# A small spread read of w_mod issued behind c on ScalarE's queue, with DMA semaphores of its own

## The chip, the cores and the metric

One core of a Trainium2 chip runs the whole block. The metric is device time in microseconds (us) of one execution. Ratios are computed from the mean time of one kernel's fast runs over that of the other's fast runs of the same rounds on the same chip, so they are not quite the ratios of the medians quoted beside them. The granted TensorE clock does not count the slow start: in the kernel before it is 1.000 although the first matmuls run at half rate until 7.7 us.

## The reference

A transformer block of a diffusion model, bf16, with two images of 256 tokens, width 1152, two heads, MLP width 4608:

```
mod = (silu(c) @ w_mod).reshape(B, 6, 1, D)          # w_mod: 1152 x 6912
shift_a, scale_a, gate_a, shift_m, scale_m, gate_m = ...
h   = layernorm(x) * (1 + scale_a) + shift_a
qkv = h @ wqkv ;  a = softmax(q k^T / sqrt(Dh)) v @ wo ;  x = x + gate_a * a
h2  = layernorm(x) * (1 + scale_m) + shift_m
out = x + gate_m * (gelu(h2 @ w_fc1) @ w_fc2)
```

## The kernel before

A small scheduler writes each engine's instructions in a fixed order and sets the semaphore waits. The parts that the change and the argument touch are the loads at the start, the way in which DMAs get semaphores, and the tensor engine's (PE's) list at the start:

```
# emit: which semaphore counts a DMA (56 in all, the last 8 for ScalarE and GpSimd)
if e == "sp":
    k = di % n_sp ; di += 1
else:
    k = n_sp + dj % n_other ; dj += 1
...
# first loads: c on ScalarE's queue, all others on SyncE's (SP)
dma(CSB[0:18, :], c.rearrange("b (k p) -> (b k) p", p=P), 18 * 256, "ld_c", eng="act")
for b in range(2):
    dma(X[:, 2*b:2*b+2, :], xv[b], ..., "ld_x%d" % b)
for (ka, kb) in ((0, KC), (KC, KT)):                  # KC = 4, KT = 9
    for k0, k1 in ((0, 3), (3, 6), (6, 9)):           # columns of scale_a
        dma(WSC[:, k0:k1, ka*P:kb*P], wmod_v[:, k0:k1, D+ka*P:D+kb*P], ..., "ld_sc%d_%d" % (ka, k0))
    for kt in range(ka, kb):
        dma(WK[:, kt, :], wqkv_v[:, kt, D:2*D], ..., "ld_wk%d" % kt)    # key weights; the first waits for x1
...
# PE at the start: 5 dummies, transpose of c, then
warm(7, "b")                                          # dummies of 512 columns
for n, behind in ((1, "bn_ln1_1_1"), (1, "aggr_ln1_1"), (2, "veps_ln1_1"), (2, "rstd_ln1_1")):
    warm(n, behind, behind)                           # dummies that also wait for x's statistics
xn_T(1); sca(0, 3); warm(1, "d"); sca(3, 6); warm(1, "f", "aggr_ln1_2")
xn_T(0); sca(6, 9); xn_T(2, 0, 8)                     # transposes of x; scale_a from w_mod's three pieces
k_first(0); k_first(1); ...                           # the first key matmuls
```

The dummies keep PE busy so that its clock rises; they compute nothing.

## Time and profile before

| | before |
|---|---|
| time, median of the first 3 runs | 244.01 us (243.94 to 244.44) |
| span of the profiled run | 242.6 us |
| PE busy | 238.3 us (98%) |
| first key matmul | 11.55 us |
| first key weights issued, landed | 6.0, 11.4 us |

The views that carry the argument stand in the prediction. In a timeline row the first number is the start in us, the second the duration, and the bracket tells how long the engine was idle and what ended that. Matmuls are pipelined and their ends are modelled, so a wait of 0.1 us between matmuls shows only in the starts. Ends of transfers come from the view of one transfer at a time ("DMA to landing"), and counts of slow packets from the trace's packet records, which no view prints.

### The profile page before, as it was taken

The page shows a single profiled execution, that of the slowest core. Times are in us where ns is not written, and L with a number is a line of the kernel's source. Part 1 is how long each engine was busy: PE and PEld are TensorE (multiplying, and loading weights), DVE is VectorE, ACT ScalarE, POOL GpSimd, SP SyncE. Part 2 cuts the span into 40 slices and gives each one's busy share as a digit, 9 for nine tenths or more (in the row PEclk, how much of TensorE's full clock was granted, in tenths as well). Part 3 has the DMA queues.
Part 4 walks back from the last instruction along what each step waited for, and adds up shares of the span by engine and source line. Part 5 has one row for each costly group of instructions (what it writes and reads, how often), then busy time and mean ns, then how long its engine had stood idle before and what let it go on. Part 6 is the DMA issues. An engine that isn't in the chain of part 4 may idle for free.

```text
span 242.6 us, 3989 instructions
## 1 busy us (share of the span) xinstructions
PE 238.3 (98%) x1717; PEld 146.4 (60%) x1727; DVE 120.0 (49%) x216; ACT 66.9 (28%) x136; POOL 21.7 (9%) x39
## 2 busy tenths in 40 slices
PE   7999999999999999999999999999999999999996
PEld 2688854557667666898444444444565665665664
DVE  3824379596988799789999600000012222211112
ACT  4730350345424207983233332222000000000000
POOL 1500000000021186400000000020000000000000
PEclk9999999999999999999999999999999999999999
DMA  6999999999994999999943488002000000000001
GB/s 237 330 383 394 388 392 389 397 412 408 390 355 138 349 385 393 390 320 394 329 145 87 165 301 331 0 16 85 0 16 19 16 16 19 16 16 16 19 17 32
DMA packets 29995, 51.57 MB, mean 213 GB/s; under 512 B 1431, under 2 KB 15643, under 8 KB 29979
## 3 DMA queue, kind: packets, MB, share of 16 engines
q1 hardware_dynamic: 29536, 50.14, 57.8%
q0 software_dynamic: 416, 1.19, 1.6%
q8 instruction: 13, 0.21, 0.4%
q14 instruction: 3, 0.02, 0.0%
q10 hardware_dynamic: 27, 0.00, 0.0%
HBM read 50.14 MB, written 1.19 MB: 212 GB/s over the span
## 4 chain that ended last, share of the span: by engine, by line
PE 98%; issue 0%; POOL 0%; DVE 0%; POOLq 0%
PE psum L688 96%; PE psum L691 2%; POOL arena L713 0%; DVE arena L1289 0%; DVE arena L1290 0%; POOL arena L712 0%; POOL arena L719 0%; POOL arena L717 0%; POOLq L1351 0%
## 5 line engine op out<-in xcount | busy, mean ns | idle before, releaser
L688 PE MATMUL psum<-arena 128*128 128x384 bf16 (+9 forms) x1628 | 235.0, 310 | 2.0 <-POOL arena L713 1.5
L688 PEld LDWEIGHTS psum<-arena 128*128 128x128 bf16 (+1 forms) x1638 | 141.1, 97 | 91.8 <-issue 4.7
L1081 DVE SCALAR_TENSOR_TENSOR arena<-arena 128x1152 f32<-128x1152 bf16 x32 | 44.7, 1413 | 0.6
L1289 DVE TENSOR_TENSOR arena<-psum,arena 128x384 f32<-128x384 f32 (+2 forms) x13 | 6.9, 527 | 68.3 <-PE psum L688 68.3
L1197 ACT ACTIVATE arena<-psum 128x512 bf16<-128x512 f32 (+1 forms) x44 | 22.4, 519 | 42.7 <-PE psum L688 42.7
L683 ACT ACTIVATE arena<-psum 128x512 bf16<-128x512 f32 (+6 forms) x37 | 19.5, 549 | 39.8 <-PE psum L688 38.5
L685 DVE CAST arena<-psum 128x512 bf16<-128x512 f32 (+3 forms) x13 | 8.1, 639 | 11.5 <-PE psum L688 11.5
L669 POOL DMA_DIRECT2D dit_scratch<-arena x3 | 1.8, 616 | 116.4 <-DVE arena L685 59.6
L1165 POOL TENSOR_TENSOR arena<-arena 128x384 f32<-128x384 f32 x12 | 10.9, 912 | 10.9 <-DVE arena L1164 9.3
L1108 DVE CAST arena<-psum 72x32 bf16<-72x32 f32 x1 | 0.2, 188 | 21.3 <-PE psum L688 21.3
L741 DVE BATCH_NORM_STATS2 arena<-arena 128x6 f32<-128x384 f32 (+1 forms) x18 | 9.5, 551 | 0.1
L1170 ACT ACTIVATE arena<-arena 128x1152 bf16<-128x1152 f32 x4 | 5.3, 1343 | 11.3 <-DVE arena L1169 11.3
L1164 DVE TENSOR_TENSOR arena<-psum,arena 128x384 f32<-128x384 f32 x12 | 6.5, 550 | 1.3 <-PE psum L688 1.2
L691 PEld LDWEIGHTS psum<-arena 128*128 128x128 bf16 (+1 forms) x89 | 5.9, 98 | 2.1 <-DMA arena<-in_c_dram 0.8
L691 PE MATMUL psum<-arena 128*128 128x128 bf16 (+1 forms) x89 | 7.1, 219 | 0.1
L1290 DVE TENSOR_TENSOR arena<-arena 128x384 bf16<-128x384 f32 (+2 forms) x13 | 6.9, 527 | 0.4
L1187 ACT ACTIVATE arena<-psum,arena 128x128 bf16<-128x128 bf16 x16 | 6.0, 455 | 1.5 <-PE psum L691 0.9
L1184 DVE TENSOR_SCALAR arena<-psum,arena 128x128 bf16<-128x128 bf16 x20 | 5.4, 336 | 1.9 <-PE psum L691 1.9
L1085 DVE STREAM_TRANSPOSE arena<-arena 128x1152 f32<-128x1152 f32 x4 | 5.5, 1368 | 0.0
L1088 DVE TENSOR_REDUCE arena<-arena 128x36 f32<-128x1152 f32 x4 | 5.4, 1346 | 0.0
L1011 ACT ACTIVATE arena<-psum,arena 128x256 bf16<-128x256 f32 x8 | 3.7, 472 | 1.3 <-PE psum L688 0.9
L745 POOL TENSOR_TENSOR arena<-arena 128x1 f32<-128x1 f32 x6 | 3.6, 596 | 1.6 <-DVE arena L744 1.6
(48 smaller groups left out, 45.3 us busy)
## 6 DMA issues: line engine op xcount, KB each, us to landing
arena<-in_w_fc_dram SPq DMA_DIRECT2D x9, 1152.0 KB, 7.1
arena<-in_w_fc_dram SPq DMA_DIRECT2D x4, 2592.0 KB, 17.4
arena<-in_wqkv_dram SPq DMA_DIRECT2D x18, 288.0 KB, 9.7
arena<-in_w_mod_dram SPq DMA_DIRECT2D x3, 1728.0 KB, 20.5
arena<-in_w_mod_dram SPq DMA_DIRECT2D x3, 864.0 KB, 13.0
arena<-in_w_mod_dram SPq DMA_DIRECT2D x9, 288.0 KB, 11.1
arena<-in_wqkv_dram SPq DMA_DIRECT2D x1, 2592.0 KB, 16.9
arena<-in_wo_dram SPq DMA_DIRECT2D x1, 2592.0 KB, 24.4
```

What stands on the lines that cost most here:

```text
L683: act(c_act(n), lambda e: e.activation(out=dst, in_=src, func=ACTF.Copy), [src], [dst], name)
L685: dve(c_dve_psum16(n) if psum16 else c_dve_psum32(n), lambda e: e.tensor_copy(dst, src), [src], [dst], name)
L688: S.instr(lambda e: e.matmul(o, lhsT=l, rhs=r, start=st, stop=sp, **kw), reads=[l, r], writes=[o])
L691: S.instr(lambda e: e.transpose(o, i_, idn), reads=[i_, idn], writes=[o])
L741: dve(550, lambda e, s=s, o=o: e.bn_stats(out=o, in_=s), [s], [o], "bn_%s_%d" % (tag, ci))
L1081: dve(1270, lambda e, w=w, s=s, acc=acc: e.scalar_tensor_tensor(out=acc, in0=w, scalar=s, in1=acc, op0=ALU.mult, op1=ALU.add), [w, s, acc] ...
L1164: dve(550, lambda e, o=o, ga=ga, x1c=x1c: e.tensor_tensor(out=x1c, in0=o, in1=ga, op=ALU.mult), [o, ga], [x1c], "wo_t1_%d_%d" % (t, ci))
L1165: S.op("pool", 930, lambda e, xs=xs, x1c=x1c: e.tensor_tensor(out=x1c, in0=x1c, in1=xs, op=ALU.add), reads=[x1c, xs], writes=[x1c], name=" ...
L1187: act(440, lambda e, o=o, dst=dst, s1=s1, s2=s2: e.activation(out=dst, in_=o, func=ACTF.Identity, scale=s1, bias=s2), [o, s1, s2], [dst], ...
L1197: act(c_act(ntok), lambda e: e.activation(out=dst, in_=o, func=ACTF.Gelu_apprx_tanh), [o], [dst], "gelu_%d_%d" % (f, tok0))
L1289: dve(c_dve_psum32(w), lambda e, o=o, gm=gm, t1=t1: e.tensor_tensor(out=t1, in0=o, in1=gm, op=ALU.mult), [o, gm], [t1], "fc2_t1_%d_%d" % ( ...
L1290: dve(c_dve_32(w), lambda e, t1=t1, x1c=x1c, ost=ost: e.tensor_tensor(out=ost, in0=t1, in1=x1c, op=ALU.add), [t1, x1c], [ost], "fc2_out_%d ...
```

## The change

Its evident intent: w_mod, the first large tensor read, was slow in its first microseconds. A tiny read of eight places 2 MB apart, by all 16 DMA engines, is to pay whatever a first touch costs before w_mod's own reads need it. It goes on ScalarE's queue, and ScalarE's two transfers get semaphores that GpSimd's do not use.

```
-        dj = 0
+        dj = da = 0
...
+                        elif e == "act":
+                            k = len(dma_sems) - 2 + da
+                            da += 1
                         else:
-                            k = n_sp + dj % n_other
+                            k = n_sp + dj % (n_other - 2)
...
         dma(CSB[0:18, :], c..., "ld_c", eng="act")
+        probe = w_mod.rearrange("(g r) f -> g r f", g=8)[:, 0, 0:512].rearrange("g (e c) -> e g c", e=16)
+        dma(sb(O_P + 3072, 64), probe, P * 64, "ld_probe", eng="act")
...
-            "act": ["ld_c", "c_tanh", ...
+            "act": ["ld_c", "ld_probe", "c_tanh", ...
```

The bytes read are never used.

More of the change, by code (lines that the diff above doesn't have):

```diff
@@ L976, in build_kernel @@
                     "hk_0_1", "hk_1_1", "hk_2_1", "hk_3_1", "hk_%d_0" % KC, "sc1a_4", "hk_%d_1" % KC] + ["hk_%d_%d" % (kt, b) for kt in range(KC + 1, KT) for b in range(2)],
-            "act": ["ld_c", "c_tanh", "sum_ln1_0", "sq_ln1_0", "sum_ln1_3", "sq_ln1_3", "xnT_cp0_4", "xnT_cp0_8", "hk_2_0", "hk_3_0",
+            "act": ["ld_c", "ld_probe", "c_tanh", "sum_ln1_0", "sq_ln1_0", "sum_ln1_3", "sq_ln1_3", "xnT_cp0_4", "xnT_cp0_8", "hk_2_0", "hk_3_0",
                     "xnT_cp1_4", "xnT_cp1_8"],
```

## The prediction

> **What bounds the kernel now.** I read the page first: engines, slices, the chain that ended last.
>
> ```profile
> span 242.6 us, 3989 instructions
> PE 238.3 (98%) x1717; PEld 146.4 (60%) x1727; DVE 120.0 (49%) x216; ACT 66.9 (28%) x136; POOL 21.7 (9%) x39
> ...
> PE   7999999999999999999999999999999999999996
> ...
> DMA  6999999999994999999943488002000000000001
> ...
> PE 98%; issue 0%; POOL 0%; DVE 0%; POOLq 0%
> ```
>
> The reader is to see that the tensor engine (PE) carries the chain almost alone; only the first slice is short of full. DMA is as full as PE for the first half, so the second reading must tell whether PE ever waits for data. A busy PE may hide small waits, because ends of matmuls are modelled, so I took the timeline of the start, where the change acts.
>
> ```profile
> 0.79 0.59 ACTq L669 DMA_DIRECT2D arena<-in_c_dram  x1
> 0.79 0.86 SPq L669 DMA_DIRECT2D arena<-in_x_dram  x2
> 1.41 1.28 ACT L728 ACT_TABLE_LOAD   x1 [1.41 <-PEq L1351]
> 1.50 2.32 PE L688 MATMUL psum<-arena 128*128 128x512 bf16 x5 [1.50 <-POOL arena L713]
> 1.70 1.63 SPq L669 DMA_DIRECT2D arena<-in_w_mod_dram  x3
> 3.74 0.10 PEld L691 LDWEIGHTS psum<-arena 18*128 18x128 bf16 x1 [0.84 <-DMA arena<-in_c_dram]
> 4.56 1.16 ACT L749 ACTIVATE arena<-arena 128x1152 bf16<-128x1152 bf16 x1 [0.40 <-DMA arena<-in_x_dram]
> 7.35 0.56 DVE L762 TENSOR_SCALAR arena<-arena 128x1152 bf16<-128x1152 bf16 x1
> ```
>
> ```profile
> 8.62 0.67 PE L691 MATMUL psum<-arena 128*128 128x128 bf16 x9
> 8.76 0.57 DVE L762 TENSOR_SCALAR arena<-arena 128x1152 bf16<-128x1152 bf16 x1
> 9.77 0.58 DVE L762 TENSOR_SCALAR arena<-arena 128x1152 bf16<-128x1152 bf16 x1
> 10.19 0.66 PE L691 MATMUL psum<-arena 128*128 128x128 bf16 x9
> 10.69 0.46 PE L688 MATMUL psum<-arena 128*128 128x2 bf16 x12
> 11.01 0.61 PE L691 MATMUL psum<-arena 128*128 128x128 bf16 x8
> 11.55 2.01 PE L688 MATMUL psum<-arena 128*128 128x256 bf16 x16
> 13.40 0.72 PE L691 MATMUL psum<-arena 128*128 128x128 bf16 x10
> ```
>
> Three normalised tiles leave DVE at 7.91, 9.33 and 10.35 us (start plus duration of the L762 rows). PE transposes them at 8.62, 10.19 and 11.01, so each was ready 0.7, 0.9 and 0.7 us early. PE is late because it must first finish its own list: 18 dummy matmuls of 512 columns, which warm its clock. Most of those before 7.7 us start 0.43 us apart, half the later rate. So x has about 0.7 us to spare.
>
> Then the weights. The view of one DMA at a time gives issue time and landing: the third piece of the attention scale (w_mod) lands at 2.8 + 7.7 = 10.5 us and is used at 10.69; the first piece of the key weights at 6.0 + 5.4 = 11.4 and the second at 6.4 + 6.0 = 12.4. From 11.01 eight transposes of 56 ns would be issued by 11.46, but the first key matmul starts at 11.55: a wait of 0.1 us. Sixteen at 109 ns would take 1.75 us, and the next row starts 1.85 us later: another 0.1. Both fit the two landings. That is all the waiting for weights I find: about 0.2 us of 244. The matmul starts after 14 us show only holes of one matmul's length (0.22 us, which fit lost records). The later traffic therefore limits nothing, however full DMA looks.
>
> What the change aims at is in the traffic of the two stretches, 5 to 10.5 us (first reads of w_mod and the key weights) and 13 to 18 us (later ones).
>
> ```profile
> DMA packets 1439, 1.70 MB, mean 308 GB/s; under 512 B 77, under 2 KB 1226, under 8 KB 1439
> ```
>
> ```profile
> DMA packets 1320, 1.90 MB, mean 379 GB/s; under 512 B 77, under 2 KB 1035, under 8 KB 1319
> ```
>
> The early stretch is 19% slower. In the packet records the 1,024-byte packets of the first w_mod reads normally take 46 ns, but 45 of 1,152 took over 74 ns, up to 674; their excess sums to 7.8 us, or 0.49 us for each of 16 engines. Packets of x show it too: the first twelve took 259 to 696 ns, later ones 178. The 1,280-byte reads of the same tensor from 13 us on have none. Something is paid on the first touch of a stretch of memory. I infer this, and no view names the mechanism.
>
> **What the Trainium skill says.** "DMA: Bandwidth & Descriptors", section "Issuing engines are not separate DMA queues", says that DMAs from scalar, sync and gpsimd run on the same 16 engines and interleave. Section "Queues, rings and completion order" of the page says that each engine goes round-robin between its queues by packet. So the probe, on ScalarE's queue, does not wait behind x; it mixes with it. The trace agrees in that packets of c start at 1.75 us and those of x at 1.80 (packet records). The same page, "Why a DMA increments its semaphore by 16 and not by 1", advises one semaphore for each transfer in flight, because early parts of another can fill the count; that is why the probe has its own, and it costs nothing. "TensorE: Matmul & The Clock Gate", section "Part 1: The HAM clock gate (the "warmup" mystery)", says that the window which decides the clock runs freely and its phase varies from run to run; the trace shows one case, 0.43 us a dummy until 7.7 us and 0.22 after. No page that I found tells of a cost of first touches.
>
> **The change part by part.** I compared the instruction order of both kernels engine by engine: PE, DVE, POOL and SP keep theirs; ScalarE has one DMA more, between c and the table load. The only other differences are semaphore numbers and one more wait, on the probe, before the exponential that writes over its landing place, tens of us later: 0.
>
> 1. Issue. The c DMA holds ScalarE's queue 0.59 us. A second one of that length ends at 0.79 + 2 x 0.59 = 1.97, so the table load of 1.28 us ends near 3.3 instead of 2.7. ScalarE's next work starts at 3.97, after c was transposed. Off the path: 0.
>
> 2. c. It stands ahead of the probe in the ring and its packets take 15 to 18 ns. Unchanged: 0, within 0.1.
>
> 3. The probe. 128 packets of 64 bytes, 8 for each engine. The 144 rows between two places are 144 x 13,824 bytes = 2.0 MB, and each engine meets all eight places. They reach the engines about 1 us after issue, near 2.4 to 2.9 us, in the middle of x. If they take over all first-touch costs of w_mod, an engine spends about 0.5 us, mixed with x. So x lands 0.3 to 0.6 us later (before: 0.8 + 3.7 = 4.5 and 1.2 + 4.7 = 5.9). The tiles have 0.7 us to spare: 0 on the path, in the middle case.
>
> 4. Return. w_mod's reads, freed of these, get up to 0.5 us shorter, so the third piece lands between the same time (all given back to x) and 0.5 earlier; I take 0.2. At 379 instead of 308 GB/s the early 1.70 MB would take 4.5 instead of 5.5 us, so 1.0 us is the upper limit. The key weights have first touches of their own (0.29 us an engine, worked out in the same way), which a probe of w_mod does not take away. They inherit the 0.2. PE can use at most the waits found above: -0.2, of which I count -0.1.
>
> Sum: 0 + 0 + 0 - 0.1. From 244.01 that gives 243.9 us.
>
> **The rivals.**
>
> A: the probe's misses block the engines and x is late by over 0.7 us. With eight misses of 0.2 to 0.3 us in a row (the usual size of the slow packets) x would be 1.6 to 2.4 us late, and PE about 0.9 to 1.7 us after the slack: 244.9 to 245.7. For it: the first packets of x took that long. Against it: w_mod has only 45 slow packets, about three an engine, not eight, and their total is 0.5 us. I give it 0.12.
>
> B: the clock rises earlier in many runs than in the profiled one. Then the dummies end sooner, PE catches up with the weights at 10.5 and 11.4 us, and an earlier landing is worth up to 0.5 to 1.0 us: 243.0 to 243.5. For it: the runs before spread from 243.94 to 244.44, as a varying phase might. Against it: none was below 243.94, and x would then bound the start. I give it 0.15.
>
> C: nothing moves, because the touched pages are not what makes the first packets slow, or the remembered places are lost by then. Then x pays a few hundredths for 128 tiny packets: 244.0, no different in the time from my middle case. 0.3.
>
> **Range and chances.** The middle is 243.9, of which A takes the upper tail and B the lower. The spread of the runs, 0.5 us, is as large as the effect. I put 243.4 to 244.6 for 8 in 10. Two per cent is 4.9 us. Nothing on this path is worth that: the whole stretch up to the first key matmul is 11.5 us, and dummies and x fill it. Faster 0.01, same 0.98, slower 0.01.
>
> **What would show it.** The profile after should show: PE's first key matmul at 11.4 to 11.5 us; the three transposes at the same times as before, within 0.1; x landing at 4.8 to 5.1 and 6.2 to 6.5; the third w_mod piece near 10.3; traffic of 5 to 10.5 us above 320 GB/s; slow packets of 1,024 bytes below 20 instead of 45; ScalarE's table load at 2.0. If x lands over 0.7 us later and the first transposes move, A was right. If the dummies change rate well before 7.7 us and the first key matmul moves earlier by more than 0.3, B was. If w_mod's packets are as slow as before, the reason given for the change is wrong and C holds. The prediction is wrong altogether if the time leaves the range while the first key matmul stands at 11.5: then something after the start moved, which I believe cannot.

## The result, and the profile after

The changed kernel takes 244.04 us (median of 6 runs, 243.93 to 244.47) and the kernel before 244.07 (6 runs, 243.83 to 244.44). The ratio is 1.0002, 95% interval 0.9989 to 1.0015. The time did not move by anything that can be measured.

The page of the changed kernel (line numbers have moved by 3 to 5), and what its third part counts on ScalarE's queue:

```profile
span 242.3 us, 4000 instructions
PE 238.6 (98%) x1727; PEld 146.5 (60%) x1727; DVE 119.8 (49%) x216; ACT 67.0 (28%) x136; POOL 21.3 (9%) x39
...
q10 hardware_dynamic: 171, 0.01, 0.0%
...
PE 99%; POOL 0%; DVE 0%; issue 0%; POOLq 0%
```

The chain is still all PE. Queue q10 is ScalarE's: 171 packets for 27 before, so the probe's 128 pieces and 16 semaphore writes are there and weigh nothing. The timeline of the start, issues first, then PE:

```profile
0.80 0.62 ACTq L672 DMA_DIRECT2D arena<-in_c_dram  x1
...
1.46 0.66 ACTq L672 DMA_DIRECT2D arena<-in_w_mod_dram  x1
...
2.15 1.28 ACT L733 ACT_TABLE_LOAD   x1 [2.15 <-issue]
```

```profile
8.41 0.67 PE L694 MATMUL psum<-arena 128*128 128x128 bf16 x9
...
9.98 0.66 PE L694 MATMUL psum<-arena 128*128 128x128 bf16 x9
...
10.80 0.61 PE L694 MATMUL psum<-arena 128*128 128x128 bf16 x8
...
11.24 2.06 PE L691 MATMUL psum<-arena 128*128 128x256 bf16 x16
...
11.76 0.11 PEld L691 LDWEIGHTS psum<-arena 128*128 128x128 bf16 x2 [0.20 <-ACT arena L686]
```

The three transposes and the first key matmul are 0.21, 0.21, 0.21 and 0.31 us earlier than before. That looks like a gain, but the first 0.21 is the clock: before, the first fast dummy starts at 7.74 us, here at 7.32, so one dummy fewer ran at 0.43 instead of 0.22 us. The other 0.1 is the wait for the first key weights, which land at 6.1 + 4.9 = 11.0 us instead of 11.4. The last row shows what is left: PE waits for a ScalarE copy, not for weights. The traffic from 5 to 10.5 us:

```profile
DMA packets 1624, 1.78 MB, mean 324 GB/s; under 512 B 226, under 2 KB 1378, under 8 KB 1624
...
q10 hardware_dynamic: 144, 0.01, 1.7%
```

Mean traffic is 324 GB/s for 308 before, and the slow packets of w_mod (1,024 bytes, over 74 ns) are 20 for 45. On these two traces alone the probe seems to do what it was made for. The second line carries a surprise: all of the probe's packets fall in this window. They run from 5.03 to 6.13 us, behind x, not among it (only six packets of x start after the first of them).

### The profile page after: what moved, and what is told of

Read it like the earlier page. It is cut to its first block, busy times and chain, and to the rows that moved or that the text cites. A ratio compares the mean times of both kernels' runs of the same rounds, so it can differ in the third digit from the quotient of the medians.

```text
span 242.3 us, 4000 instructions
## 1 busy us (share of the span) xinstructions
PE 238.6 (98%) x1727; PEld 146.5 (60%) x1727; DVE 119.8 (49%) x216; ACT 67.0 (28%) x136; POOL 21.3 (9%) x39
## 4 chain that ended last, share of the span: by engine, by line
PE 99%; POOL 0%; DVE 0%; issue 0%; POOLq 0%
PE psum L691 96%; PE psum L694 2%; POOL arena L718 0%; DVE arena L1294 0%; DVE arena L1295 0%; POOL arena L717 0%; POOL arena L724 0%; POOL arena L722 0%; POOLq L1356 0%
## 5 line engine op out<-in xcount | busy, mean ns | idle before, releaser
L691 PE MATMUL psum<-arena 128*128 128x384 bf16 (+7 forms) x1638 | 235.6, 310 | 1.5 <-POOL arena L718 1.5
L688 DVE CAST arena<-psum 128x512 bf16<-128x512 f32 (+3 forms) x13 | 8.2, 640 | 11.5 <-PE psum L691 11.5
## 6 DMA issues: line engine op xcount, KB each, us to landing
arena<-in_w_mod_dram SPq DMA_DIRECT2D x9, 288.0 KB, 11.1
```

Source lines behind the costliest of these rows:

```text
L688: dve(c_dve_psum16(n) if psum16 else c_dve_psum32(n), lambda e: e.tensor_copy(dst, src), [src], [dst], name)
L691: S.instr(lambda e: e.matmul(o, lhsT=l, rhs=r, start=st, stop=sp, **kw), reads=[l, r], writes=[o])
```

## The experiments

Theory P: the probe takes over first-touch costs of w_mod, weights land earlier, and PE's own list hides it. Rival N: the better landings are chance. Rival S: any small transfer ahead of w_mod does the same. Rival C, from the prediction: nothing that matters moves.

**before_again: the kernel before, profiled once more.** No edit.

> The kernel before, unchanged, to see what a second profile of it shows by chance. Both theories: ratio 1.000 within 0.15%. Theory P (the probe really warms w_mod): again 40 to 50 of the 1,152 packets of 1,024 bytes over 74 ns, their excess about 0.5 us an engine, and the first key-weight piece lands near 11.4 us. Rival N (the better landings after were chance): the count or the landing comes as low here as in the changed kernel, 21 packets and 11.0 us. Theory L (the time is the tensor engine's own list) also expects: if the clock rises one dummy earlier or later than at 7.7 us, the first key matmul and the whole span move by 0.21 us with it.

Measured: 243.98 us, ratio 1.0003 (0.9986 to 1.0019). Timeline rows, and the traffic from 5 to 10.5 us:

```profile
10.65 0.62 PE L691 MATMUL psum<-arena 128*128 128x128 bf16 x8
11.12 1.98 PE L688 MATMUL psum<-arena 128*128 128x256 bf16 x16
```

```profile
DMA packets 1569, 1.99 MB, mean 362 GB/s; under 512 B 94, under 2 KB 1246, under 8 KB 1569
```

Without any probe there are now 21 slow packets, the first key weights land at 6.2 + 4.8 = 11.0 us, traffic is 362 GB/s, and the first key matmul starts at 11.12 us, earlier than with the probe. The clock rose at 6.46 us. Theory P's evidence falls: two traces of the same kernel differ by as much as before and after.

**same_place: the probe reads one stretch of 0.1 MB.**

```
-probe = w_mod.rearrange("(g r) f -> g r f", g=8)[:, 0, 0:512].rearrange("g (e c) -> e g c", e=16)
+probe = w_mod[0:8, 0:512].rearrange("g (e c) -> e g c", e=16)
```

> The probe reads 128 pieces of 64 bytes from the first eight rows of w_mod, one stretch of 0.1 MB, not eight places 2 MB apart. Theory P: only the first stretch is touched, so the slow packets come back, 38 to 46 over 74 ns and 0.4 to 0.5 us an engine, and the first key-weight piece lands at 11.3 to 11.6 us. Rival S (any small transfer ahead of w_mod does it): 18 to 25 slow packets and 11.0 us as with the spread probe. On where the probe runs: if it starts at 5.0 us because its first touches take 3 us to answer, it would now start earlier, near 2.5 us; if the queues are served in the order of issue, again at 5.0. Time in both: 244.0 within 0.15%.

Measured: 244.01 us, ratio 1.0006 (0.9991 to 1.0021). Slow packets 15, first key weights at 11.08 us, probe packets from 5.22 to 6.09 us. Spreading the places buys nothing over one place. The probe runs at 5.2 us here too, so it is not held up by its own touches.

**other_tensor: the same spread probe on w_fc1**, whose first other read is issued at 52 us.

```
-probe = w_mod.rearrange(...)
+probe = w_fc1.rearrange(...)
```

> The same spread probe on w_fc1, which nothing reads before some 60 us. Theory P: the cost without the gain: slow packets of w_mod 40 to 50, first key-weight piece 0.3 to 0.6 us later than the kernel before, at 11.7 to 12.0 us, and the first key matmul as much later as that lies behind the list: up to 0.5 us, ratio 1.000 to 1.002. Rival S: 18 to 25 slow packets and 11.0 us.

Measured: 243.99 us, ratio 1.0001 (0.9986 to 1.0016). Slow packets 23, first key weights at 11.20 us, first key matmul at 11.34. In these profiles it matters little which tensor is touched. The expected delay of 0.3 to 0.6 us against the kernel before did not come; against before_again of the same chip it is 0.2.

**probe_first: the probe ahead of c on ScalarE's queue.**

```
-            "act": ["ld_c", "ld_probe", "c_tanh", ...
+            "act": ["ld_probe", "ld_c", "c_tanh", ...
```

> On ScalarE's queue the probe is issued ahead of c, so it reaches the engines together with x and not behind it. If the queues are served in the order of issue (theory O), its packets start at 1.8 us, x lands 0.4 to 0.8 us later (4.9 to 5.3 and 6.4 to 6.8), and c, issued second, comes between the halves of x or behind them, so that the transpose of c moves from 3.75 to about 4 to 6 us and the tensor engine loses up to 2 us there. If queues take turns (what the prediction held), c lands within 0.5 us of before, and x up to 0.8 us later. Time: 244.0 to 246.

Measured: 246.81 us, ratio 1.0122 (1.01 to 1.0145). The timeline, then q10 in the window from 3.6 to 4.3 us:

```profile
6.11 0.19 PE L694 MATMUL psum<-arena 18*128 18x18 bf16 x1 [2.29 <-DMA arena<-in_c_dram]
```

```profile
q10 hardware_dynamic: 144, 0.01, 13.8%
```

The probe's packets run from 3.69 to 4.18 us, after the first half of x, and c, issued at 1.46, from 5.28 us, after the second. The transpose of c moves from 3.75 to 6.11 us, and the dummies behind it run slow until 10.5 us, so the first key matmul starts at 14.10. The loss of 2.8 us is c's delay. x lands when it did before (4.5 and 6.0 us): my expected 0.4 to 0.8 us later did not come. x's first half and the probe were issued at the same 0.80 us here, so this run does not tell which of two transfers issued together goes first. The place of c, ahead of the probe or behind it, is the one thing about this small probe that cost a measurable time.

**few_before and few_after: four dummies less, without and with the probe.** If PE's list hid the probe's gain, it would show here.

```
-        warm(7, "b")
+        warm(3, "b")
```

> The kernel before with four dummy matmuls less behind the transpose of c (3 for 7). Theory L (the tensor engine's own list of dummies, each 0.43 us until the clock rises and 0.22 after, holds back the start, with x 0.2 to 0.9 us behind it): the first transpose comes when its tile is ready, at 7.9 to 8.2 us instead of 8.2 to 8.6, and the first key matmul at 11.0 to 11.2 us, whatever the phase of the clock; time 0.1 to 0.4 us less, ratio 0.9985 to 1.000. If the weights bound (they land at 11.0 to 11.4): no gain at all where they land late. A loss of over 0.3 us would say that fewer dummies delay the rise of the clock.

> The changed kernel with the same four dummies less. If the probe brings weights earlier and only the list hid it (the prediction's picture), this is 0.2 to 0.5 us faster than the same without the probe: its first key-weight piece lands 0.3 to 0.5 us before that one's. If the probe does nothing (theory N, after the first four experiments), both land and run alike: key weights within 0.2 us, times within 0.15%.

Measured on one chip: 244.35 us (ratio to the kernel before 1.0018, 1.0002 to 1.0035) and 244.55 us (1.0025, 1.0009 to 1.0042). Timelines of the one without and the one with the probe:

```profile
10.87 0.61 PE L691 MATMUL psum<-arena 128*128 128x128 bf16 x8
11.46 1.91 PE L688 MATMUL psum<-arena 128*128 128x256 bf16 x16
```

```profile
10.97 0.61 PE L694 MATMUL psum<-arena 128*128 128x128 bf16 x8
11.49 1.92 PE L691 MATMUL psum<-arena 128*128 128x256 bf16 x16
```

The first key weights land at 11.32 and 11.35 us, and in both the first key matmul follows 0.14 us later. Here the weights are the bound, and with the probe they come no earlier, though its slow packets are 14 and not 36. That is the direct test of theory P's use, and it fails: one profile of each shows no earlier weights, and the six timed runs of each show no gain (their means differ by 0.17 us, the one with the probe slower). Nor is dropping dummies a gain: 0.1 to 0.4 us less was expected, 0.4 more was measured. The timed runs of both lie between 243.83 and 245.20 us, half of them at 244.6 and over. A clock that rises later when PE idles between dummies would fit, but the profiled runs are of the faster kind (span 242.4), so this is argued and not shown. No fall of the clock in mid-run was recorded: the granted clock is 1.000 in all twelve, where such a fall in "twice" below gives 0.986.

**more_before: four dummies more** (11 for 7).

> The kernel before with four dummies more (11 for 7). Theory L: each goes straight into the time once the list is the bound, at 0.215 us after the clock rises: 0.5 to 0.9 us more (less where the clock rises early and x had been the bound), ratio 1.002 to 1.0035; the weights and x land as before, and no wait for weights is left at the first key matmul. If x or the weights set the start, less than 0.2 us more.

Measured: 244.22 us, ratio 1.0007 (0.9992 to 1.0021), where I expected 1.002 to 1.0035. The clock rose at 6.0 us; the list ends at 11.56 us and the first key matmul starts there. In such a run the kernel before is held by x or the weights until about 11.1 to 11.3 us, so of 0.86 us of added dummies only an estimated 0.2 to 0.4 show (the medians differ by 0.26). The picture of one bound, PE's list, was too simple: list, x and weights lie within half a microsecond of each other.

**twice: w_mod's first three pieces read twice from the same addresses**, first to an unused place.

```
+        AGAIN = wmat(O_R, KC * P)
+        for k0, k1 in ((0, 3), (3, 6), (6, 9)):
+            dma(AGAIN[:, k0:k1, :], wmod_v[:, k0:k1, D:D + KC * P], ..., "ld_again%d" % k0)
```

> The kernel before, but the three pieces of 384 KB of w_mod are read twice from the same addresses, first to an unused place, then as always. It is 2 to 4 us slower, as the weights come 3.3 to 4.3 us later. Theory F (a first touch of each stretch of memory costs): the first reading has 20 to 45 packets over 74 ns, the second fewer than 5, and the key weights behind them again have 15 to 30 over 150 ns. Rival H (the slow packets belong to the first 10 us or so of the program, whatever is read): the second reading, up to about 11 us, has 15 or more slow packets, and the key weights, now read from about 12 us on, few.

Measured: 249.46 us (one run, state unknown), 5.5 us slower and not 2 to 4. Traffic from 5 to 9, 9 to 12.5 and 13 to 17 us:

```profile
DMA packets 1159, 1.24 MB, mean 309 GB/s; under 512 B 54, under 2 KB 1130, under 8 KB 1159
```

```profile
DMA packets 1214, 1.22 MB, mean 348 GB/s; under 512 B 50, under 2 KB 1194, under 8 KB 1214
```

```profile
DMA packets 946, 1.55 MB, mean 388 GB/s; under 512 B 73, under 2 KB 516, under 8 KB 946
```

Of 68 slow packets, 25 start after 9.2 us, about where the second reading begins, at addresses read microseconds earlier. The key weights, never touched before, have one packet over 150 ns, where the kernel before has 28. Both go against theory F: fewer than 5 and 15 to 30 were expected. First touch of an address does not explain the slow packets, though the second reading has fewer than the first (43).

The time beyond the forecast is the clock's. PE's timeline and the page's row of the granted clock (slices of 6.2 us):

```profile
11.77 0.92 PE L688 MATMUL psum<-arena 128*128 128x2 bf16 x13 [2.79 <-DMA arena<-in_w_mod_dram]
...
15.90 3.30 PE L688 MATMUL psum<-arena 128*128 128x256 bf16 x16
...
PEclk9959999999999999999999999999999999999999
```

PE stood idle for 2.79 us, and from 11.91 to 18.73 us the granted clock was 0.50, so that the first key matmuls start 0.21 us apart instead of 0.11. That is worth an estimated 2.2 us: 0.9 before the first key matmul (the weights would have allowed 14.98) and 1.3 behind it (232.3 us for 231.0).

**late_start: the kernel before, held back by a memset of 8.7 us**, to ask whether they follow the program's start or the stream's.

```
+        HOLD = sb(O_R, 20736)
+        S.op("pool", 9000, lambda e: e.memset(HOLD, 0.0), writes=[HOLD], name="hold")
         for b in range(2):
             dma(X[:, 2 * b:2 * b + 2, :], xv[b], ..., "ld_x%d" % b)
+            S.instrs[-1].deps.update(j for j in S.instrs if j.name == "hold")
```

> The kernel before, held back by one long memset of GpSimd (5 to 12 us) before x, w_mod and the weights may be issued; everything moves by that much and the time grows by it. If the slow packets belong to the first 12 us or so of the program, the w_mod reads (now from 11 to 17 us on) have fewer than 8 packets over 74 ns, and the key weights fewer than 5 over 150 ns. If they belong to the first 6 us or so of a stream of loads, whenever it starts, there are 20 to 45 and 15 to 30 again.

Measured: 253.19 us (one run, state unknown). There are 63 slow packets of w_mod and 24 of the key weights, from 13.9 us on. They move with the stream, and not with the program's start: w_mod and the key weights alike have them.

```profile
19.67 0.61 PE L691 MATMUL psum<-arena 128*128 128x128 bf16 x8
20.43 0.81 PE L688 MATMUL psum<-arena 128*128 128x256 bf16 x6 [0.15 <-DMA arena<-in_wqkv_dram]
```

Here the wait is long enough for the profile to name it: the key weights, landed at 20.3 us.

**probe_late: the probe issued behind the tanh of c**, at 3.98 us.

```
-            "act": ["ld_c", "ld_probe", "c_tanh", ...
+            "act": ["ld_c", "c_tanh", "ld_probe", ...
```

> The probe is issued behind the tanh of c, near 4.2 us: after all three first w_mod pieces are issued (3.3 us) and before the key weights (6.0 us). If the DMA engines served all queues in the order of issue, its packets would come behind the third w_mod piece, at about 9 to 10 us. If they take turns between the queues, one transfer's share at a time (which also fits where it ran so far: behind x, or between the halves of x when it was issued first), they come within the w_mod pieces, at 5.3 to 7.5 us. ScalarE's first statistics start about 0.4 us later. Time 244.0 within 0.5 us.

Measured: 244.08 us (one run, state unknown). q10 in the window from 8 to 9.8 us:

```profile
q10 hardware_dynamic: 144, 0.01, 5.4%
```

The packets run from 8.11 to 9.67 us, beside the end of the third w_mod piece (last packet 9.77 us, issued at 3.1) and before most of the key weights (issued at 6.2 us, first packet 8.43, on whichever engine was ready). Taking turns would have put them at 5.3 to 7.5 us. The order of issue across the two queues fits this run and the ones before. The packet records do not tell the engine, so this is the order of all packets together, not that of one engine.

**probe8: the suspected cost eight times over**, 1,024 pieces of 64 places.

```
-probe = w_mod.rearrange("(g r) f -> g r f", g=8)[:, 0, 0:512].rearrange("g (e c) -> e g c", e=16)
-dma(sb(O_P + 3072, 64), probe, P * 64, "ld_probe", eng="act")
+probe = w_mod.rearrange("(g h r) f -> g h r f", g=8, h=8)[:, :, 0, 0:512].rearrange("g h (e c) -> e g h c", e=16)
+dma(sb(O_P + 3072, 512).rearrange("p (h c) -> p h c", h=8), probe, P * 512, "ld_probe", eng="act")
```

> The probe eight times as large: 1,024 pieces of 64 bytes of 64 places, 64 for each engine. At 11 ns a packet an engine is busy with it 0.7 us instead of 0.09, and the issue on ScalarE's queue is longer than 0.65 us. If touching w_mod does help and the eight places were only too few, slow packets of w_mod fall below 8 and its third piece lands as early as before in spite of the cost; otherwise 15 to 45 slow ones, and w_mod and the key weights land 0.6 to 1.5 us later than without a probe, the first key matmul at 11.8 to 12.6 us, time 0.5 to 1.4 us more (ratio 1.002 to 1.006).

Measured: 244.54 us, ratio 1.0017 (1.0000 to 1.0034). PE's timeline:

```profile
9.91 0.70 PE L691 MATMUL psum<-arena 128*128 128x2 bf16 x13 [0.40 <-DMA arena<-in_w_mod_dram]
...
11.27 0.47 PE L691 MATMUL psum<-arena 128*128 128x2 bf16 x12 [0.15 <-DMA arena<-in_w_mod_dram]
...
12.11 1.25 PE L691 MATMUL psum<-arena 128*128 128x256 bf16 x10
```

PE now waits for w_mod by name, and the first key weights land at 11.98 us, 0.85 later than in before_third (11.13, same chip). Slow packets are 23: more places do not help. The cost is real. If it is linear, which was not tested, 0.85 us for 64 packets an engine is 13 ns each (one packet takes 11 in the records), so an estimated 0.11 us for the eight of the change, on weights that are only sometimes the bound.

**shared_sems: the change without its second part.**

```
-                        elif e == "act":
-                            k = len(dma_sems) - 2 + da
-                            da += 1
                         else:
-                            k = n_sp + dj % (n_other - 2)
+                            k = n_sp + dj % n_other
```

> The changed kernel without the second part of the change: semaphores dealt out as before, so that the transfers of ScalarE and of GpSimd share the last eight. The check may refuse it, because a GpSimd transfer then counts on a semaphore that c's transfer has raised to 16 before; then the semaphores of its own are what makes the probe possible and no matter of speed. If it runs: time and profile as the changed kernel's, 244.0 within 0.15%.

The check refused it: a GpSimd transfer would use a semaphore that "must start at 0" while c's transfer had raised it to 16. It did not run. The Trainium skill's "DMA: Bandwidth & Descriptors", section "Rules for kernel authors", asks the same: a DMA's semaphore must be 0 at first use. With nine transfers on eight semaphores the deal wraps, and GpSimd's last transfer falls on c's semaphore. In the changed kernel GpSimd's seven transfers on six semaphores wrap too, onto one of their own, and that was accepted. So the semaphores of its own for ScalarE are what makes the extra transfer legal; a matter of speed was not seen, as this kernel could not run.

**before_third: the kernel before once more**, for what was still open.

> The kernel before once more, for the one question left open: slow packets of 1,024 bytes were 45, 21, 36 and 25 in runs without a probe and 14 to 28 in runs with any probe, wherever it reads. If any small transfer ahead of w_mod makes them fewer (rival S), there are 30 or more again; if the count is only scatter, it may as well be 14 to 28. In both, the first key matmul is the later of two: the list's end, and the landing of the first key weights plus 0.12 us, within 0.03 us; the span is that plus 231.0, within 0.15 us.

Measured: 243.94 us, ratio 0.9996 (0.998 to 1.0013), slow packets 53, first key matmul 11.31 us, span 242.35.

**All starts together.** From the timelines: the end of PE's list is the start of the third group of transposes plus eight of 0.056 us. It takes in PE's earlier waits for x and w_mod, so that in probe8 the list itself ends late because w_mod does. The 0.12 us between a landing and the matmul are read from these timelines.

| run | first fast dummy | list ends | key weights + 0.12 | first key matmul | span | span less matmul |
|---|---|---|---|---|---|---|
| before | 7.74 | 11.46 | 11.54 | 11.55 | 242.55 | 231.0 |
| before_again | 6.46 | 11.10 | 11.11 | 11.12 | 242.09 | 231.0 |
| before_third | 7.62 | 11.32 | 11.25 | 11.31 | 242.35 | 231.0 |
| few_before | 4.6 | 11.32 | 11.44 | 11.46 | 242.35 | 230.9 |
| more_before | 6.00 | 11.56 | 11.20 | 11.56 | 242.70 | 231.1 |
| changed kernel | 7.32 | 11.25 | 11.12 | 11.24 | 242.29 | 231.1 |
| few_after | 4.75 | 11.42 | 11.47 | 11.49 | 242.41 | 230.9 |
| same_place | 5.1 | 11.18 | 11.20 | 11.22 | 242.19 | 231.0 |
| other_tensor | 5.86 | 11.28 | 11.32 | 11.34 | 242.28 | 230.9 |
| probe_late | 7.60 | 11.30 | 11.13 | 11.30 | 242.35 | 231.1 |
| probe8 | 5.5 | 12.05 | 12.10 | 12.11 | 243.01 | 230.9 |
| probe_first | 10.8 | 14.11 | 10.50 | 14.10 | 245.16 | 231.1 |

In every row the first key matmul is the later of the two columns before it, within 0.02 us, and 231 us follow. (late_start fits too: weights 20.42, matmul 20.43, span 251.43. twice does not: 232.3 us follow its matmul at 15.90, because the clock was at half until 18.73.) Chance alone, in when the clock rises and when the weights land, moves the first key matmul of the unchanged kernel by 0.43 us in three profiles; the probe's estimated cost is 0.11.

**What stays open.** Slow packets were 45, 21, 36, 25 and 53 in five runs without a probe, 63 in late_start, and 20, 15, 23, 28, 14, 16 and 23 in seven with one. There may be fewer behind any small transfer, wherever it reads: the 53 of before_third are what rival S said (30 or more). Against it, probe_late has only 16, and there the probe's first packet comes after 870 of the 1,152. The ranges overlap, and the first key weights land at 11.42, 10.99, 11.32, 11.08, 11.13 without and 11.00, 11.08, 11.20, 11.35, 11.01 with a probe of 128 pieces behind c, a mean of 11.19 and 11.13. What makes the packets at the start of a stream slow is not settled, nor how long it lasts: in more_before 35 packets of 1,280 bytes took over 90 ns for a usual 55, the last at 18.2 us.

## Why the prediction was right or wrong

The time was right: 243.9 us in 243.4 to 244.6 was said, 244.04 was measured. It could hardly tell the middle case from rival C, which lie 0.1 us apart, so it is no support for the mechanism, and that was wrong. The two reasons for "same" held: PE works through its list without large holes, and nothing after the first key matmul moves (231.0 us in twelve runs). The rest by its own steps:

- **Step 1, issue.** Right. The table load starts at 2.15 us for the 1.97 to 2.0 said, and ScalarE's next work at 3.98 for 3.97.
- **Step 2, c.** Right: its transpose is at 3.75 us as before.
- **Step 3, the probe amid x.** Wrong, and the mechanism behind it: I held that ScalarE's queue mixes with SP's. The probe ran after x, from 5.03 to 6.13 us and not at 2.4 to 2.9, and x landed at 4.4 and 6.0 us, not at 4.8 to 5.1 and 6.2 to 6.5. (The landings alone decide nothing: in before_again x landed at 4.8 and 6.2 us without a probe.) The cost fell on w_mod instead (a slot that probe8 sizes at an estimated 0.11 us).
- **Step 4, the return of 0.1 us.** Wrong in its cause. The third piece landed at 3.0 + 7.3 = 10.3 us and traffic rose to 324 GB/s, as said, but the kernel before reached 10.25 us and 362 GB/s by itself in before_again. The term is 0 within 0.15%. Of the two waits, only the first was for weights alone: the second is in part PE waiting for ScalarE to empty accumulator banks, and it stayed (16 key matmuls take 1.90 us in the changed kernel, 1.85 before) though the second key weights landed 0.4 us earlier.
- **Semaphores.** I took transfers in flight as the reason for the probe's own. shared_sems shows another: without it the check refuses the program.
- **"First touch"**, which I inferred from the slow packets, falls with twice: the second reading is slow again and the untouched key weights are not.
- **Signs.** Three missed: the transposes moved by 0.21 us and not within 0.1, the first key matmul came at 11.24 and not at 11.4 to 11.5, and slow packets were 20 and not below. The clock and the first key weights explain the first two.
- **Rival A** did not come. **Rival B** is half right: the clock does rise early in many runs, and then x and the weights hold the start at 11.1 to 11.3 us, as its objection said; its 243.0 to 243.5 us came in no run. **Rival C** is what holds: the reason for the change was wrong. I gave it 0.3, and it did not differ from my middle case in the time. Its sign, packets as slow as before, was not seen in the changed kernel's profile (20 for 45); only the second profile of the kernel before showed that 45 was one draw of many.

## What to carry to other kernels

Profile the unchanged kernel twice before believing that a change moved a landing by 0.4 us: here two profiles of one kernel differ as much as before and after. Write a start as the later of its few inputs (here list and weights), because a gain on one of several near-equal inputs gives almost nothing. Keep the small transfer that all else waits for first on its queue: putting 8 KB ahead of c cost 2.8 us.

## What the Trainium skill lacked or had wrong

- "DMA: Bandwidth & Descriptors", section "Queues, rings and completion order": by its round-robin between queues, a small transfer on ScalarE's queue would take turns with SP's. In these runs it came where its issue time put it: issued at 0.80, 1.46 and 3.98 us, it ran at 3.69 to 4.18, 5.03 to 6.13 and 8.11 to 9.67 us, behind what SP had issued earlier or, in the first case, at the same time. The three cases fit an order of issue. Whether the engines' turns or the making of the descriptors keeps it was not isolated, so the page need not be wrong about the turns themselves.
- "TensorE: Matmul & The Clock Gate", section "Part 1: The HAM clock gate (the "warmup" mystery)", tells of a transition that varies by 500 ns either way from run to run, and further on of 6, 11 or 14 slow matmuls in one kernel. Here PE starts its dummies at 1.50 us in each, and the first fast one starts between 4.6 and 7.7 us, after 7 to 14 slow ones, in runs whose list is the same up to there. The second figure fits, and the 500 ns are too few.
- No page that I found tells that the first 10 us or so of a stream of loads have slow packets, whichever of the tensors they read: 21 to 63 of 1,152 packets of 1,024 bytes over 74 ns for a usual 46 in six profiles without a probe, and none of the 1,280-byte reads from 13 us on in the first trace (but 35 of 1,152 in more_before).
